# A block of unread matmuls of whole, half and quarter height behind the last rows of a routing-attention and GLU kernel

## The chip, the cores and the metric

The kernel runs on one core of one Trainium2 chip. The metric is the device time of one execution in microseconds. A profiled execution also has a span, from its first to its last instruction, which is a little shorter than its time.

## The reference, cut to what matters

Clustered attention is followed by a gated feed-forward layer. B = 4, H = 8, S = 768, D = 64, 16 clusters per head, d_ff = 1536:

```python
q_assign = argmax(einsum('bhsd,hcd->bhsc', q_n, c_n), -1)   # q_n, c_n: of length one
k_assign = argmax(einsum('bhsd,hcd->bhsc', k_n, c_n), -1)
mask = q_assign[:, :, :, None] == k_assign[:, :, None, :]
scores = where(mask, scale * q @ k.T, -1e9)
attn = softmax(scores) @ v                                  # [4, 8, 768, 64]
x = attn.transpose(0, 2, 1, 3).reshape(3072, 512)
out = (sigmoid(x @ w_gate) * (x @ w_val)) @ w_out           # [3072, 512]
```

The added block computes nothing of this: it multiplies zeros by zeros, and nothing reads what it writes.

## The kernel before, in words

Work goes batch by batch, and in each batch head by head. For a block of 128 keys and 384 queries, `do_scores` (L535) makes one matmul of 80 rows, 64 of the head's dimension and 16 of the cluster's one-hot code, into a PSUM tile `sc`; ScalarE takes the exponent into `es` (L546); `do_av` (L549) makes three matmuls 65 columns wide into `av` (L558), the 65th column being the sum. `normalise` (L290) divides on VectorE and GpSimd. The heads of a batch form `xT`, on which the feed-forward layer works in blocks of 384 rows (`ffn_atoms`, L388): for each of 12 slices of d_ff four matmuls into `g` (L397) and four into `v` (L412), 384 columns wide; then for each 128 rows 12 matmuls into `o` (L429). VectorE and ScalarE empty these tiles.

The order of all engines is that in which the Python code issues the instructions. A table `SCHED` says at which step a piece of background work is issued, `ffn_run` (L506) takes feed-forward pieces from a queue by a credit of nanoseconds per step. After the last head, `ffn_run(1e9)` empties the queue, and the last block of 384 rows of the last batch is computed alone, with `final=True`. Its last 128 rows are made by `closing` (L449 and on), in column parts of 256, 128 and 128, each of 12 matmuls into a tile `o_end` (L453), emptied by ScalarE (the first part, L462) and VectorE (the others, L460) into `ob_end` and stored by SP (L463). That is the end of the kernel before; the change stands behind it.

PSUM tiles of one bank come from `bank` (L130), a pool `ring` of four buffers, taken in turn. `g`, `v`, `sc` and `o_end` use it. The last four tiles of the ring before the change are the last `v` and the three `o_end`. A pool makes the first write of a new tile wait until the buffer's previous tile has been written and read for the last time.

Behind the program SP waits for all queues and engines whose last work nothing else has waited for, and all engines meet in two rounds of a barrier.

Of the kernel before, what the change touches and what calls it, by code (L numbers as in the profile page):

```python
# [9 lines left out]
HP = mybir.dt.float16  # L10
# [64 lines left out]
def kernel(  # L75
# [430 lines left out]
    def ffn_run(ns):  # L506
        credit[0] += ns
        while queue and credit[0] > 0:
            c, f = queue.pop(0)
            credit[0] -= c  # L510
            f()
        if not queue:
            credit[0] = min(credit[0], 0.0)
# [522 lines left out]
    ffn_block(xT, 384, 384, B - 1, CH[1], True)  # L1036
    ffn_run(1e9)


# [1 line left out]
_INS = ['q', 'k', 'v', 'centroids', 'moe_w_gate', 'moe_w_val', 'moe_w_out']  # L1041
# [26 lines left out]
```

## Time and profile before

| what | value |
|---|---|
| time, median of 2 runs | 338.64 us (338.25 to 339.03) |
| time of the profiled execution | 338.76 us |
| its span | 336.6 us |
| mean granted clock of TensorE | 0.99 |
| TensorE matmuls in the span | 3422, busy 327.1 us |
| LDWEIGHTS | 3422, busy 210.8 us |

PE is TensorE's matmuls, PEld its weight loads, DVE VectorE, ACT ScalarE, POOL GpSimd, SP the engine that issues most transfers; a name with a q behind it is that engine's instruction queue. A line of a timeline or group gives the start and the busy time in microseconds, the engine, the source line, the operation, what it writes and reads, shapes, and how many instructions are merged (x4). In brackets stand the idle time before and what ended it. The duration of a single matmul covers its whole way through the pipe; how often one can start is seen from the starts of neighbours.

### The profile page before, as it was taken

Reading aid. Unit: us, or ns where it says so; the run is one execution under the profiler, and the core shown is the slowest. Engines: PE = TensorE matmul, PEld = TensorE weight load, DVE = VectorE, ACT = ScalarE, POOL = GpSimd, SP = SyncE. Lnnn points to the kernel's source line nnn. Section 1 sums busy time; section 2 is a strip of 40 time slices with the busy share of each in tenths; the row PEclk is TensorE's granted clock in tenths of the full one; section 3 lists DMA queues with packets and bytes.
Section 4 is the critical chain, followed back from the end, with each engine's and each line's share of the span. In section 5 each row is a group of like instructions: output and inputs, shape, how many; then the busy total and the mean of one; then the engine's idle time right before and its main releaser. Section 6 shows DMA issues by size and latency. Waiting matters only on the chain.

```text
span 336.6 us, 9001 instructions
## 1 busy us (share of the span) xinstructions
PE 327.1 (97%) x3422; PEld 210.8 (63%) x3422; DVE 187.6 (56%) x530; ACT 236.4 (70%) x543; POOL 109.3 (32%) x151
## 2 busy tenths in 40 slices
PE   7798999999999999999999999999999999999996
PEld 4686866766666666666556665666556655654654
DVE  6668755796567777465646664466534331340431
ACT  6587987766899888877768776787777876532321
POOL 6668454442254444513242333313201010100000
PEclk9789999999999999999999999999999999999999
DMA  7999989744795969597457755872622022101002
GB/s 205 360 159 129 204 207 188 105 148 91 239 236 106 229 167 237 148 193 196 90 180 168 189 92 116 234 114 49 130 72 47 14 25 74 46 0 64 32 0 95
DMA packets 80523, 45.25 MB, mean 134 GB/s; under 512 B 57376, under 2 KB 77536, under 8 KB 80480
## 3 DMA queue, kind: packets, MB, share of 16 engines
q1 hardware_dynamic: 74400, 39.83, 49.3%
q0 software_dynamic: 5792, 4.72, 9.9%
q8 instruction: 27, 0.44, 0.6%
q14 instruction: 16, 0.13, 0.1%
q10 hardware_dynamic: 288, 0.13, 0.1%
HBM read 28.34 MB, written 6.29 MB: 103 GB/s over the span
## 4 chain that ended last, share of the span: by engine, by line
PE 86%; DMA 5%; DVE 3%; POOL 2%; issue 2%; SPq 1%; ACT 0%; POOLq 0%; DVEq 0%
PE v L412 18%; PE g L397 18%; PE o L429 17%; PE sc L541 17%; PE av L558 9%; DMA qraw<-in_q_dram 3%; PE lg L335 2%; DMA T<-hl 2%; PE lg L326 1%; PE t_ps L720 1%; POOL hl L708 1%; PE o_end L453 1%; POOL wv L198 1%; PE oh_ps L757 1%; DVE hT L417 1%
## 5 line engine op out<-in xcount | busy, mean ns | idle before, releaser
L546 ACT ACTIVATE es<-sc 128x384 f16<-128x384 f32 x384 | 173.5, 492 | 43.2 <-PE sc L541 26.1
L541 PE MATMUL sc<-T 80*128 80x384 f16 x384 | 118.6, 330 | 0.7 <-DVE T L775 0.2
L558 PEld LDWEIGHTS <-es 128*128 128x128 f16 x1152 | 82.6, 98 | 45.6 <-issue 1.5
L558 PE MATMUL av<-va,es 128*128 128x65 f16 x1152 | 98.1, 194 | 0.0
L417 DVE SCALAR_TENSOR_TENSOR hT<-th,v 128x384 f16<-128x384 f32 x96 | 53.1, 553 | 71.7 <-PE av L558 47.4
L397 PE MATMUL g<-xTb,wg 128*128 128x384 f16 x384 | 78.1, 325 | 0.2
L412 PE MATMUL v<-xTb,wv 128*128 128x384 f16 x384 | 78.1, 325 | 0.0
L429 PE MATMUL o<-wo,hT 128*128 128x512 f16 x276 | 68.7, 378 | 0.0
L299 POOL TENSOR_TENSOR xp<-t,rec 128x192 f16<-128x192 f32 (+1 forms) x46 | 29.1, 633 | 116.7 <-DVE rec L296 76.9
L403 ACT ACTIVATE th<-g 128x384 f32<-128x384 f32 x96 | 47.2, 491 | 25.4 <-DVE hT L417 16.2
L397 PEld LDWEIGHTS <-wg 128*128 128x128 f16 x384 | 37.2, 97 | 21.7 <-issue 1.1
L412 PEld LDWEIGHTS <-wv 128*128 128x128 f16 x384 | 37.2, 97 | 21.0 <-issue 0.7
L429 PEld LDWEIGHTS <-hT 128*128 128x128 f16 x276 | 26.8, 97 | 23.5
L541 PEld LDWEIGHTS <-T 80*128 80x128 f16 x384 | 37.3, 97 | 0.8 <-DVE T L775 0.6
L957 POOL TENSOR_TENSOR hl<-kraw,hl 128x384 f16<-128x384 f32 x22 | 20.4, 927 | 34.4 <-DVE hl L956 18.3
L294 DVE TENSOR_TENSOR t<-av,sv 128x195 f32<-128x195 f32 (+1 forms) x46 | 20.1, 436 | 20.4 <-PE av L558 19.7
L957 POOL TENSOR_TENSOR hl<-qraw,hl 128x384 f16<-128x384 f32 x22 | 20.1, 912 | 21.1 <-DVE hl L956 21.1
L438 ACT ACTIVATE ob<-o 128x512 f32<-128x512 f32 x15 | 9.0, 597 | 12.4 <-PE o L429 12.1
L349 DVE TENSOR_TENSOR lgs<-lg,lglo 128x192 f32<-128x192 f32 x22 | 7.8, 356 | 14.6 <-ACT lglo L341 14.2
L436 DVE TENSOR_SCALAR ob<-o 128x512 f32<-128x512 f32 x8 | 5.5, 690 | 16.8 <-PE o L429 16.8
L248 POOL CAST va<-vraw 128x768 f16<-128x768 f32 x16 | 13.5, 848 | 0.2 <-DMA vraw<-in_v_dram 0.2
L335 PE MATMUL lg<-cm,T 128*128 128x32 f16 x264 | 10.0, 177 | 0.4 <-DMA T<-hl 0.4
(112 smaller groups left out, 248.9 us busy)
## 6 DMA issues: line engine op xcount, KB each, us to landing
vraw<-in_v_dram SPq DMA_DIRECT2D x16, 384.0 KB, 5.4
out_dram<-ob SPq DMA_DIRECT2D x23, 256.0 KB, 2.2
kraw<-in_k_dram SPq DMA_DIRECT2D x15, 384.0 KB, 3.9
qraw<-in_q_dram SPq DMA_DIRECT2D x12, 384.0 KB, 4.1
wg<-in_moe_w_gate_dram POOLq DMA_DIRECT2D x4, 384.0 KB, 5.6
wv<-in_moe_w_val_dram POOLq DMA_DIRECT2D x4, 384.0 KB, 5.8
wo<-in_moe_w_out_dram POOLq DMA_DIRECT2D x2, 768.0 KB, 11.2
qraw<-in_q_dram SPq DMA_DIRECT2D x7, 192.0 KB, 6.8
```

The costliest lines, as they stand in the source:

```text
L294: DVE.tensor_tensor(t[:, 0:nq, :], av, sv, ALU.add)
L299: (eng or POOL).tensor_tensor(x, t[:, 0:nq, 0:64], bcast(rec[:, 0:nq], 64), ALU.mult)
L335: PE.matmul(out=lg[:, bass.ts(c, 32)], lhsT=t[:, c, :], rhs=cm[:, h].rearrange("p s n -> p (s n)"), start=True, stop=True,)
L397: PE.matmul(out=g[:, 0:n], lhsT=wg[fc // WQ][:, dc, fc % WQ, :], rhs=xT[:, dc, t0 : t0 + n], start=(dc == 0), stop=(dc == NDC - 1),)
L403: ACT.activation(th[:, 0:n], g[:, 0:n], AF.Tanh, scale=0.5)
L412: PE.matmul(out=w[:, 0:n], lhsT=wv[fc // WQ][:, dc, fc % WQ, :], rhs=xT[:, dc, t0 : t0 + n], start=(dc == 0), stop=(dc == NDC - 1),)
L417: DVE.scalar_tensor_tensor(hT[:, fc, 0:n], st[0][:, 0:n], 1.0, w[:, 0:n], ALU.add, ALU.mult)
L429: PE.matmul(out=o, lhsT=hT[:, fc, bass.ts(t, 128)], rhs=wo[fc // 6][:, fc % 6, :], start=(fc == 0), stop=(fc == NFC - 1),)
L541: PE.matmul(out=sc.rearrange("p (c t) -> p c t", t=128), lhsT=s["k"], rhs=s["q"], start=True, stop=True,)
L546: ACT.activation(es, sc, AF.Exp, scale=SCALE)
L558: PE.matmul(out=av[:, s["c0"] + i, :], lhsT=s["es"][:, bass.ts(i, 128)], rhs=VA[b, p][:, e, s["j"], :], start=(first and i == 0), stop=(la ...
L957: POOL.tensor_tensor(hl[:, :, 64:128], r, hl[:, :, 0:64], ALU.subtract)
```

## The change

Behind the last row block a tile `sw` of 128x384 fp16 zeros is made by GpSimd, and 96 matmuls 384 columns wide are issued on TensorE, each with a weight load of its own, 128 columns wide. A helper `put(t, r0, n)` takes `n` rows of `sw` from row `r0`. With fewer than 128 rows it gives the position of the rows in the array; the built program then has tiles of 64x128 (64 rows) or 32x128 (16 rows) at that position, and 128x128 for the whole ones. `banks` takes the four buffers of the ring anew, so t[i] is always the same bank. SP's closing waits get one on TensorE's last count, third from last. Nothing else differs in the order of any engine.

```diff
@@ -1036,6 +1036,51 @@
     ffn_block(xT, 384, 384, B - 1, CH[1], True)
     ffn_run(1e9)
 
+    sw = const.tile([128, 384], HP, name="sw")
+    POOL.memset(sw, 0.0)
+
+    def put(t, r0, n, start=True, stop=True):
+        kw = dict(tile_position=(r0, 0)) if n < 128 else {}
+        PE.matmul(
+            out=t[:, 0:384], lhsT=sw[r0 : r0 + n, 0:128], rhs=sw[r0 : r0 + n, 0:384],
+            start=start, stop=stop, skip_group_check=True, **kw,
+        )
+
+    def banks(name):
+        return [bank(512, name=name) for _ in range(4)]
+
+    t = banks("p_full")
+    for i in range(8):
+        put(t[i % 4], 0, 128)
+    t = banks("p_two")
+    for i in range(8):
+        put(t[i % 2], 64 * (i % 2), 64)
+    t = banks("p_four")
+    for i in range(8):
+        put(t[i % 4], 32 * (i % 4), 16)
+    for j in range(3):
+        t = banks("p_mix")
+        for i in range(4):
+            put(t[i], 64 * (i % 2), 64, True, False)
+        for i in range(4):
+            put(t[i], 32 * i, 16, False, True)
+        t = banks("p_gap")
+        for i in range(4):
+            put(t[i], 0, 128)
+    for j in range(3):
+        t = banks("p_weave")
+        put(t[0], 0, 64, True, False)
+        put(t[1], 64, 64, True, False)
+        put(t[0], 64, 16, False, True)
+        put(t[1], 96, 16, False, True)
+        put(t[2], 0, 64, True, False)
+        put(t[3], 64, 64, True, False)
+        put(t[2], 0, 16, False, True)
+        put(t[3], 32, 16, False, True)
+        t = banks("p_gap2")
+        for i in range(4):
+            put(t[i], 0, 128)
+
```

The first matmul of a tile in a bank waits as the pool says: in p_full the second for ScalarE's and the third and fourth for VectorE's emptying of an `o_end`; from p_two on for TensorE's own last matmul in that bank's previous tile that was written.

## The prediction

> **What bounds the kernel now.** I read the page's shares first, then the chain of waits, then the last six microseconds as a timeline, and last the rows of TensorE that can price the new matmuls. The shares and the slices (PE row, then the granted clock):
>
> ```profile
> PE 327.1 (97%) x3422; PEld 210.8 (63%) x3422; DVE 187.6 (56%) x530; ACT 236.4 (70%) x543; POOL 109.3 (32%) x151
> ...
> PE   7798999999999999999999999999999999999996
> ...
> PEclk9789999999999999999999999999999999999999
> ```
>
> TensorE is busy from the second slice to the last, at full clock from the fourth on. Whatever is put behind its last matmul finds no free TensorE time inside the span; it can only use the tail. The chain of waits over the last part, merged:
>
> ```profile
> 323.74 0.65 PE v L412 x4
> 324.39 0.65 PE g L397 x4
> 325.04 0.65 PE v L412 x4
> 325.69 5.18 PE o L429 x24
> 330.87 2.66 PE o_end L453 x36
> 333.53 0.02 issue
> 333.56 0.29 DVE ob_end L460
> ```
>
> Until 333.5 us the chain is TensorE alone. Four matmuls 384 wide take 0.65 us, 162 ns each, from start to start, weight loads included. The tail, in the timeline:
>
> ```profile
> 330.70 2.81 PE L453 MATMUL o_end<-wo,hT 128*128 128x256 f16 x36
> ...
> 332.22 0.38 ACT L462 ACTIVATE ob_end<-o_end 128x256 f32<-128x256 f32 x1 [3.30 <-PE o_end L453]
> 332.62 1.58 SPq L463 DMA_DIRECT2D out_dram<-ob_end  x3
> 332.89 0.29 DVE L460 TENSOR_SCALAR ob_end<-o_end 128x128 f32<-128x128 f32 x1 [1.29 <-PE o_end L453]
> 333.56 0.29 DVE L460 TENSOR_SCALAR ob_end<-o_end 128x128 f32<-128x128 f32 x1 [0.38 <-PE o_end L453]
> ```
>
> The last matmul ends at 333.52, DVE empties its bank until 333.85, the last store is issued at 333.88 and lands about 1.5 us later, and SP's closing waits and two barrier rounds end the span at 336.62. Closing rows:
>
> ```profile
> L1063 SPq EVENT_SEMAPHORE  x11: 17/28/28, 334.3 to 336.6; - x11
> ...
> L1063 SPq DRAIN  x3: 7/7/7, 335.8 to 336.1; - x3
> ```
>
> So 3.1 us lie between TensorE's last matmul and the end of the span.
>
> Prices of short matmuls, and of a change in the number of rows:
>
> ```profile
> 68.15 0.75 PE L326 MATMUL lg<-cm,T 128*128 128x16 f16 x24
> ...
> 142.24 0.33 PE L541 MATMUL sc<-T 80*128 80x384 f16 x1
> 142.41 0.81 PE L397 MATMUL g<-xTb,wg 128*128 128x384 f16 x4
> ```
>
> Twenty-four pairs of weight load and matmul, 16 columns wide, take 0.75 us; less 0.17 for the last one's own length that is 25 ns a pair, so issue costs at most that. An 80-row matmul is followed by a 128-row one after 0.17 us, hardly more than the 162 of the same width: a change in the number of rows alone costs a few ns. A 384-wide matmul lasts 325 ns in its group's row, twice its spacing: the pipe holds 163 ns more than the streaming.
>
> **The change part by part.** Nothing is removed or moved; the order of every engine before the block is the same. POOL gets one memset of 128x384 behind its last xp product; POOL is idle from 300 us on (0.00 busy in the windows from there), so TensorE's first load of sw finds it done: nothing. DVE, ACT and the DMA queues get nothing. SP gets a wait on TensorE's last count, in the third-last of its closing waits. What costs is 96 pairs of load and matmul on TensorE: 32 of 128 rows (8 p_full, 12 p_gap, 12 p_gap2), 32 of 64 rows (8 p_two, 12 p_mix, 12 p_weave) and 32 of 16 rows (8 p_four, 12 and 12), all 384 wide. None can start before the last o_end matmul, at 333.30, so p_full starts at 333.36 (55 ns on, the spacing of 128-wide ones).
>
> *Whole ones*: 162 ns each, the row above. *Halves and quarters*: no row shows two matmuls in different rows of the array. They cost between 25 ns (issue) and 162 ns (each for itself). They are set on disjoint rows and, side by side, in different banks, so I take two halves, or four quarters, per 162 ns, the later ones 25 ns behind: 81 and 41 ns each, between the ends. [...]
>
> *Switches between whole, half and quarter*: 26 of them in the block. Below, 0 (the 80-row row); above, 0.20 us (a full completion, 325 ns plus the 37 ns from TensorE's end to DVE's start above, less the 162 that passes anyway). A new cut of the array is nearer to a part of the pipe emptying than to a shorter operand, but loads and fetches of the next one overlap in all rows, so I take 0.10, the middle. [...]
>
> *Waits of TensorE on itself*: each first use of a bank waits for the last matmul in that bank's previous tile. Start to start this is 0.36 us (0.325 + 0.037). It binds only where that matmul was in the slot just before: p_two to p_four, p_four to the first p_mix, and p_mix to p_gap three times; there it takes the switch's place.
>
> Sums, from first start to the next group's first start:
> - p_full: 8 x 0.162, and 0.05 as the fourth bank is released by DVE at 333.85 + 0.04: 1.35; with the switch 1.45.
> - p_two: the last slot starts at 0.49, and p_four waits 0.36 for it: 0.85.
> - p_four: second slot at 0.16, plus 0.36: 0.52.
> - p_mix: two slots and the 25 ns offset 0.35, switch 0.10, self-wait 0.36: 0.81. p_gap: 0.65 + 0.10 = 0.75. Three times 1.56 = 4.68.
> - p_weave: four slots with offset and switch, 4 x (0.162 + 0.025 + 0.10) = 1.15; p_gap2 0.75. Three times 1.90 = 5.69; less 0.26, as the last group counts only to its last start.
>
> Together 12.93 us (1.45 counted with its switch), last start at 346.29, end and signal 0.36 later at 346.65. Behind it stand two SP waits or drains and the barrier: from SP's place in the old order to the end of the span 0.95 us (rows 0.06 apart up to the drains at 335.8, then 0.8). The span becomes 347.6, 11.0 more than 336.6. The profiled execution took 338.76, 2.14 more than its span (and 0.12 above the median 338.64 of the two runs): 349.7 us. The stores are done at 335.4 and are off the path.
>
> **The rivals.**
> - *No price for a switch*: with 0 to 0.05 us the self-waits alone remain, and the times are 347.1 to 348.7. For it: the 80-row row. Against it: that row keeps one cut of the array.
> - *A switch empties everything*: 0.16 (325 less 162) to 0.25 us (loads held back too) gives 351.2 to 353.5. For it: TensorE lasts 325 ns per matmul, and a new cut may have to see the last column out. Against it: loads run far ahead in every row. [...]
> - *Tiles do not run beside each other*: 88 matmuls behind p_full at 162 ns each, 14.3 us, give 352.3 without a switch's price and 355 with 0.10. For it: nothing in this trace shows sharing, and all stream 384 columns into full-width banks. Against it: the positions are disjoint.
> - *Not slower, within 2%*: 2% is 6.8 us, about what a measurement of this kernel can tell from no change. If tiled matmuls went at the issue row's 25 ns, the block would be 32 x 162 + 64 x 25 = 6.8 us, and the time some 343.5 (the tail hides about 2). It decides below 52 ns per tiled matmul, on average, switches and waits included. Against it: halves stream 384 columns, and two rows of 64 fill the array.
>
> **How the numbers follow.** Forecast (sharing, switch 0.05 to 0.16, 348.7 to 351.2): 0.40. No price: 0.22. Emptying: 0.17. No sharing: 0.18. Within 2%: 0.03. The range 347.0 to 353.2 takes in the first two, most of the third and the cheap half of the fourth; about 0.15 is left out. All but the last are slower by over 2% (above 345.4): 0.96; within 0.03; faster 0.01, as nothing is taken away.
>
> **What would show it.** p_two's starts in pairs some 25 ns apart and 162 ns between pairs: sharing; an even 162: none. From the last p_gap to the first p_weave half, 0.26 us is my switch, 0.16 none, 0.32 or more emptying. From a p_mix quarter to the p_gap in its bank, 0.36. The block should run from 333.36 to about 346.6 with the clock at 1.00. Wrong would be: other switch costs, loads of tiles that can't run ahead, or a late start (sw's memset, a bank).

## The result, and the profile after

The changed kernel takes 348.96 us (347.68 and 350.24, two runs) against 338.64: ratio 1.0307, 95% interval 1.0257 to 1.0356. Run once more, beside other kernels, it took 348.70 (four runs) against 337.40: 1.0345, 1.0304 to 1.0386. The ratios and intervals are taken over fast runs alone, so they need not be the quotients of the medians beside them. The forecast was 349.7, slower, in a range of 347.0 to 353.2. The profiled execution of after took 347.68, its span 345.5.

First the page of after, with TensorE's share, its slices and the granted clock:

```profile
PE 338.4 (98%) x3518; PEld 215.1 (62%) x3518; DVE 186.7 (54%) x530; ACT 236.1 (68%) x543; POOL 109.9 (32%) x152
...
PE   7899999999999999999999999999999999999998
...
PEclk9899999999999999999999999999999999999999
```

96 matmuls more, at full clock (1.00 in the stretch from 331.5 to 344.6 us). The second and third slices of the granted clock stand apart from the profile of before (9 8 9 9 against 9 7 8 9): the clock was granted at half for 3.4 us early on here and for 6.8 us there, so the old work ended 1.79 us sooner in this execution. That is not the change. Measured from 0.056 us behind the start of the last o_end matmul, where the first new one starts, the comparison is clean: from there the span of before has 3.26 us to go, that of after 13.98. The block costs 10.7 us; the forecast had 11.0.

The chain of waits of after, its last part (start, length, what; the views write p_gap2 as p_gap):

```profile
329.08 2.65 PE o_end L453 x36
331.73 1.35 PE p_full L1044 x8
333.08 0.76 PE p_two L1044 x8
333.84 0.57 PE p_four L1044 x8
334.40 0.74 PE p_mix L1044 x8
335.15 0.01 issue
335.15 0.81 PE p_gap L1044 x4
...
339.08 1.07 PE p_weave L1044 x8
340.16 0.76 PE p_gap L1044 x4
```

The chain now runs through the block to its last matmul. Eight halves take 0.76 us where eight whole ones take 1.35. The wait lists of after, of the engines and of SP's queue, from 331 us on (waiter, releaser, us in total, times, longest), and behind them SP's wait in the kernel before:

```profile
PEld L1044 <- issue: 6.0, 26, 0.3
```

```profile
SPq L1108 <- PE p_gap L1044: 10.7, 1, 10.7
SPq L1108 <- DMA out_dram<-ob_end: 1.0, 2, 0.6
```

```profile
SPq L1063 <- DMA out_dram<-ob_end: 1.0, 3, 0.6
```

TensorE's load side stood 26 times, once per switch between whole, half and quarter, 6.0 us in all: inside p_full a load starts 0.16 us ahead of its matmul or more, the first one behind a switch 4 to 5 ns, and 0.12 us where the matmul of p_gap waits for a bank. SP, whose stores were long on their way, waited 10.7 us for TensorE's last count; before, it waited for the stores. A stretch of the timeline shows the groups:

```profile
331.51 1.18 PEld L1044 LDWEIGHTS <-sw 128*128 128x128 f16 x8
331.56 1.52 PE L1044 MATMUL p_full<-sw 128*128 128x384 f16 x8
331.76 0.29 DVE L460 TENSOR_SCALAR ob_end<-o_end 128x128 f32<-128x128 f32 x1 [0.38 <-PE o_end L453]
333.01 0.44 PEld L1044 LDWEIGHTS <-sw 64*128 64x128 f16 x8 [0.32 <-issue]
333.01 0.82 PE L1044 MATMUL p_two<-sw 64*128 64x384 f16 x8
```

The length of a group is its starts plus the last matmul's own 0.33. For p_two that leaves 0.49 us, three slots between four pairs; for p_full 1.19, seven slots and 0.06 of waiting for VectorE. The first load of p_two begins with its first matmul, where the first load of p_full began before it. In the trace the two of a pair of p_two start 3 to 4 ns apart.

### The profile page after: what moved, and what is told of

Same layout as the page of the kernel before. It is cut to its first block, busy times and chain, and to the rows that moved or that the text cites. A ratio compares the mean times of both kernels' runs of the same rounds, so it can differ in the third digit from the quotient of the medians.

```text
span 345.5 us, 9195 instructions
## 1 busy us (share of the span) xinstructions
PE 338.4 (98%) x3518; PEld 215.1 (62%) x3518; DVE 186.7 (54%) x530; ACT 236.1 (68%) x543; POOL 109.9 (32%) x152
## 4 chain that ended last, share of the span: by engine, by line
PE 89%; DMA 3%; POOL 2%; DVE 2%; issue 1%; ACT 1%; POOLq 0%; DVEq 0%; SPq 0%; ACTq 0%
PE v L412 17%; PE o L429 17%; PE g L397 17%; PE sc L541 16%; PE av L558 9%; DMA T<-hl 3%; PE lg L335 2%; PE p_gap L1044 1%; PE t_ps L720 1%; PE lg L326 1%; PE wm L604 1%; PE p_weave L1044 1%; POOL hl L708 1%; PE o_end L453 1%; PE p_mix L1044 1%
## 5 line engine op out<-in xcount | busy, mean ns | idle before, releaser
L403 ACT ACTIVATE th<-g 128x384 f32<-128x384 f32 x96 | 47.2, 492 | 25.4 <-DVE hT L417 16.2
```

Source lines behind the costliest of these rows:

```text
L403: ACT.activation(th[:, 0:n], g[:, 0:n], AF.Tanh, scale=0.5)
```

## The experiments

Each leaves the 3072x512 result as it is and changes only the block that nobody reads. The block's length is from p_full's first start (or that of what stands in its place) to the last start; it is 12.68 us in both profiles of the changed kernel. It is read from the trace, since whole times move by up to 3.7 us (before: 336.08 to 339.74), most of it with the clock of the first 20 us (0.83 there in the profile of before, 0.91 in that of after, 1.00 behind in both; at a mean granted clock of 1.00 the kernel before took 336.08 to 337.43, at 0.99 337.83 to 339.74).

**All tiled matmuls on the same rows.**

```diff
-        kw = dict(tile_position=(r0, 0)) if n < 128 else {}
+        kw = dict(tile_position=(0, 0)) if n < 128 else {}
-            lhsT=sw[r0 : r0 + n, 0:128], rhs=sw[r0 : r0 + n, 0:384],
+            lhsT=sw[0:n, 0:128], rhs=sw[0:n, 0:384],
```

> The same 96 matmuls, but every half and every quarter stands on the rows from 0, so that no two use different rows; tile sizes, switches and waits stay. Forecast's account (tiles of one size on different rows share a slot of 0.162 us): the sharing is gone, p_two lasts 8 x 0.162 instead of 4, the block from p_full's first start to the last start 18.1 us instead of the 12.7 of the changed kernel, the time about 5.4 us more than the changed kernel's. Rival (the paired starts are only records, each matmul has its own time in any case): block 12.7 us, no difference. Starts within a group 0.162 apart by the first account, 3 to 4 ns apart by the second.

Measured: 365.05 us, ratio 1.081 (1.0749 to 1.0872), block 28.2 us: neither account. Its timeline:

```profile
332.17 1.47 PE L1044 MATMUL p_two<-sw 64*128 64x384 f16 x8
333.57 1.47 PE L1044 MATMUL p_four<-sw 16*128 16x384 f16 x8
334.97 1.57 PE L1044 MATMUL p_mix<-sw 64*128 64x384 f16 x8
336.47 1.44 PE L1044 MATMUL p_gap<-sw 128*128 128x384 f16 x4
337.85 2.85 PE L1044 MATMUL p_mix<-sw 64*128 64x384 f16 x8
```

and its stretches before and after 336.5 us (stretch, its length, busy time and count of PE, PEld, DVE, ACT, POOL, then the granted clock, the share of the DMA engines and GB/s):

```profile
330.60:336.50 5.90, 5.90 (x38) 2.76 (x36) 0.29 (x1) 0.00 (x0) 0.00 (x0) 1.00 0.14 46
336.50:360.00 23.50, 22.94 (x65) 5.76 (x64) 0.00 (x0) 0.00 (x0) 0.00 (x0) 0.50 0.00 0
```

Up to 336.5 the first account holds: p_two has seven slots (1.47 less 0.33) instead of three, the starts are 0.162 apart. So the sharing is in the time, not only in the records. Behind that the granted clock is 0.50, and the starts within a group are 0.32 apart: from 337.85 to 340.63 p_mix takes 2.78 us, where from 334.97 to 336.47 it took 1.50. That was in neither account and is taken up below.

**Sorted by size.**

```diff
...
+    t = banks("p_full")
+    for i in range(32):
+        put(t[i % 4], 0, 128)
+    t = banks("p_two")
+    for i in range(32):
+        put(t[i % 4], 64 * (i % 2), 64)
+    t = banks("p_four")
+    for i in range(32):
+        put(t[i % 4], 32 * (i % 4), 16)
```

> The same numbers of matmuls, 32 whole, 32 halves, 32 quarters, sorted by size: 2 switches instead of 26 and hardly a wait on itself. Forecast's account: 32 + 16 + 8 slots of 0.162 and 2 x 0.10, block 9.3 us from first to last start, time 3.4 us below the changed kernel's. Rival (no price of a switch, only the five self-waits and the order cost something): the block loses 1.0 us at most. Rival without sharing: block 15.5 us, longer than now.

Measured: block 9.35 us, 3.34 below the changed kernel's. Time 346.08, ratio 1.0247 (1.0203 to 1.0291), below the 1.0345 of the second measurement of the changed kernel, on another chip. The timeline:

```profile
333.83 5.42 PE L1044 MATMUL p_full<-sw 128*128 128x384 f16 x32
339.18 2.77 PE L1044 MATMUL p_two<-sw 64*128 64x384 f16 x32
341.88 1.61 PE L1044 MATMUL p_four<-sw 16*128 16x384 f16 x32
```

The same 32 of each: 5.35, 2.71 and 1.29 us to the next group or to the last start. Here halves cost half, quarters a quarter. The 3.34 us are 24 switches (some 2.5), the quarters that p_weave puts in twos instead of fours (3 slots, 0.49), and for the rest waits.

**Whole and half in turn.**

```diff
...
+    t = banks("p_alt")
+    for i in range(96):
+        put(t[i % 4], 0, (128, 64)[i % 2])
```

> 96 matmuls, whole and half in turn, all from row 0, over four banks without any new tile: 95 switches, no wait on itself. Forecast's account: 96 x 0.162 + 95 x 0.10, block 24.9 us from first to last start, 0.262 between neighbours, time some 12.2 us above the changed kernel's. Rival (a switch costs nothing by itself; what was seen are self-waits or the pool): block 15.4 us. Rival (a switch empties the whole pipe, 0.325 from start to start): 30.9 us.

Measured: block 25.4 us, 0.265 to 0.270 from start to start behind the first pair, clock 1.00; 362.11 us, ratio 1.071 (1.0654 to 1.0767).

```profile
330.53 25.71 PE L1044 MATMUL p_alt<-sw 128*128 128x384 f16 x96
```

Ninety-five switches at 0.105: the price is that of the switch, with no wait in sight, and far from the 0.163 by which a matmul's 0.325 exceeds its slot. A load of its own is not enough for it: halves that follow halves on the same rows start 0.162 apart (p_two of the first experiment).

**Ten whole ones only**, with nothing behind them.

```diff
-    for i in range(8):
+    for i in range(10):
         put(t[i % 4], 0, 128)
...
```

> The block cut to ten whole matmuls, which end some 1.9 us behind the last row's matmul, while the last store is still on its way. Forecast's account: the last of them is counted before SP comes to its wait for TensorE, the time is that of the kernel before, within 0.3 us. Rival (the end of the kernel hangs on TensorE, or the matmuls delay the last emptying or store): 1.5 us more than before.

Measured: 338.47 against 337.72, ratio 1.0008 (0.9974 to 1.0041). From the last o_end matmul's start to the end of the span 3.34 us, in before 3.32. SP's wait is that of before, for the stores:

```profile
SPq L1080 <- DMA out_dram<-ob_end: 1.0, 3, 0.6
```

The tail holds ten matmuls for nothing.

**The changed kernel again.**

> The changed kernel once more, beside the three others. By every account the block lasts 12.7 us from first to last start; the span differs by how long the clock stays at half near the beginning (0 to 6.8 us in the runs so far), so the time lies between 346 and 350.5 us.

Measured: 348.70 us (346.68 to 349.96), block 12.68.

**Other banks for the gaps.** p_gap and p_gap2 write tiles of the pools avp and op in turn.

```diff
-        t = banks("p_gap")
+        t = others("p_gap")
...
-        t = banks("p_gap2")
+        t = others("p_gap2")
```

> p_gap and p_gap2 write four banks of the two other PSUM pools, so that p_gap no longer waits for the quarter just before it. Forecast's account (0.39 us from start to start is the wait on itself, 0.10 the bare switch): from the first quarter of a p_mix to its p_gap 0.26 to 0.27 us instead of 0.39, block 12.3 us. Rival (going from quarters back to whole ones is a dearer switch, whatever the bank): 0.39 stays, block 12.7.

Measured: block 12.39; from the first quarter to p_gap 0.26 to 0.27 us instead of 0.39, three times. The wait on itself was the rest.

**128 columns wide.**

```diff
-            out=t[:, 0:384], lhsT=sw[r0 : r0 + n, 0:128], rhs=sw[r0 : r0 + n, 0:384],
+            out=t[:, 0:128], lhsT=sw[r0 : r0 + n, 0:128], rhs=sw[r0 : r0 + n, 0:128],
```

> All 96 matmuls 128 columns wide instead of 384, so a slot is 0.056 us. Forecast's account, taken as a fixed price: still 0.10 for each switch, so from the last whole one to the first half 0.16 us, and 0.28 for a wait on itself; block 7.0 to 7.3 us. Rival (the price grows with the width streamed): 0.03 for a switch, 0.09 from start to start, block 5.5 us or less.

Measured: block 7.04. In p_weave the first half starts 0.150 behind the last whole one, the first quarter 0.162 behind the first half, p_gap2 0.161 behind the first quarter: 0.10 over the 0.055 slot, as with three times the width. Between 128 and 384 columns the price did not grow with the width.

**Loads of 64 columns.**

```diff
-            out=t[:, 0:384], lhsT=sw[r0 : r0 + n, 0:128], rhs=sw[r0 : r0 + n, 0:384],
+            out=t[0:64, 0:384], lhsT=sw[r0 : r0 + n, 0:64], rhs=sw[r0 : r0 + n, 0:384],
```

> All weight loads 64 columns instead of 128 (outputs on 64 partitions), the same width of 384, rows and order. What the switch's price is made of: a fixed 0.10 by the forecast as it stands, block 12.7 us. If it is the way of the last column across the array, 64 array columns fewer shorten it by some 64 slots of 0.42 ns (162 ns for 384), that is by 0.027 to 0.07. If it is a weight load that can't run ahead, it changes with the load's own length, up or down.

Measured: block 12.90. From whole to half 0.255 (0.258 before), in p_weave from the last half to the first quarter 0.277 (0.265), and the second matmul behind a switch starts 0.183 behind the first instead of 0.170. Nothing is shortened beyond 3 ns, where the account of the last column needed 27 at least, so the price did not follow the columns loaded; 13 ns are added where a load cannot run ahead, and the loads themselves last longer (medians of 103 ns with 64 columns, 93 with 128). So part of the price, by an estimate about 10 of 100 ns (0.170 less the usual 0.159 to 0.162), is likely the load; what the other 90 are made of was not shown.

**Why the clock fell.** Three kernels, one execution each: 96 halves from row 0, 96 matmuls of 16 rows from row 0, and the first experiment with weights of the output layer in place of zeros. Their lines in this order:

```diff
+        put(t[i % 4], 0, 64)
...
+        put(t[i % 4], 0, 16)
...
+            lhsT=wo[0][0:n, 0, 0:128], rhs=wo[1][0:n, 0, 0:384],
```

> 96 halves, all from row 0, over four banks: one switch, no sharing. In the run with all tiled matmuls from row 0 the granted clock fell to half some 4.4 us into the block, with about 40 of 128 rows in use on average. Account (the clock is granted by how much of the array is at work; whole and half in turn, with 59 of 128 rows on average, kept it): 64 of 128 rows keep the clock, starts stay 0.162 apart, block 15.4 us. Rival (any long stretch of tiled matmuls without sharing loses the clock): starts 0.32 apart from some 4 us on, block 25 us or so.

> 96 matmuls of 16 rows, all from row 0: one switch, no sharing, 16 of 128 rows in use. Account (clock by the share of the array at work): the clock falls to half within 3.4 to 7 us, starts 0.162 apart before and 0.32 behind, block 23 to 28 us. Rival (the fall was caused by the many switches there): block 15.4 us at full clock.

> The kernel with all tiled matmuls from row 0 once more, with weights of the output layer in place of zeros in both operands. Account (the clock is granted by the rows at work, whatever they hold): it falls to half as with zeros, block 26 to 30 us. Rival (it fell because the operands were zeros): the clock stays, block 18.1 us, starts 0.162 apart in each group and 0.26 at a switch.

Measured: halves 15.4 us at full clock to the end; 16 rows 27.1 us; with weights 27.6 us. The timeline groups of the first two, and the second's granted clock in slices:

```profile
332.59 15.77 PE L1044 MATMUL p_same<-sw 64*128 64x384 f16 x96
```

```profile
332.71 27.59 PE L1044 MATMUL p_same<-sw 16*128 16x384 f16 x96
```

```profile
PEclk9699999999999999999999999999999999999655
```

The clock fell 3.45 us after the first 16-row matmul, and 4.4 and 4.9 us after the first lone half in the kernels with zeros and with weights. So neither zeros nor switches do it (with 95 switches it stayed at 1.00); the kernels of halves and of 16-row matmuls differ in the rows, and so in the tile, alone, and only the second lost the clock.

The clock's steps stand on a grid: in the 16-row kernel at 5.06, 11.89, 18.72 and 336.16 us, which are 2, 2 and 93 stretches of 3.413 us; in the trace of before 2 such stretches at half are followed by 93 at full (6.827 and 317.440 us), in that of after 1 by 97 (3.413 and 331.093). The grid does not stand still against the program: its first recorded step is at 5.87 us in before and at 6.16 in after. So the time from a start to the fall is partly chance: the 16-row matmuls began 0.03 us before such a stretch. An estimate from the starts in these traces: averaged over the last whole stretch before the fall, gaps of the switches included, some 30 of 128 rows were in use in the first experiment, 44 in that with weights and 16 in the 16-row kernel; 56 to 59 (whole and half in turn) and 64 (halves) kept the clock. At half clock, by the same count, a mean of up to 75 rows, each matmul counted for its 0.320 us, did not bring it back. Whether and where a limit lies, whether the mean is taken over such a stretch, and whether a 16-row matmul counts as 16 rows or as the 32 of its tile, wasn't tried. Being busy was not enough here: TensorE was at work for 22.94 of 23.50 us, by the second of the two stretches of the first experiment, and the clock stayed at half.

## Why the prediction was right

- *Nothing fits beside the old work, only the tail is free*: right. p_full began 0.056 us behind the last o_end matmul, 0.055 forecast, and ten whole matmuls cost nothing (ratio 1.0008).
- *p_full 1.35, with the switch 1.45*: 1.45 measured, the wait for VectorE included.
- *Sharing*: right, shown by the two kernels that take it away (starts 0.162 apart) and sort it (2.71 and 1.29 us for 32). The 25 ns offset was too much: it is the spacing of the 24 pairs of load and matmul in the prediction's row, all on the same 128 rows; on different rows the partner starts 3 to 4 ns behind. In four p_weave slots this is the largest miss: 1.07 measured, 1.15 forecast, three times, 0.23 in all. The 41 ns for a quarter in fours held: behind the first ones four start per 0.162 us.
- *The switch, 0.10, taken between 0 and 0.20*: 0.095 behind whole ones, 0.093 behind the halves of p_mix, 0.102 behind halves and quarters of p_weave. The choice had no row of its own; that it fell on the middle was luck. The price was paid even where the rows that a matmul needs lay idle: in p_weave the half on rows 0 to 63 starts 0.263 behind the second quarter, on rows 96 to 111, and 0.53 behind the last use of its own rows. It was less than a wait until the last matmul is through: 0.263 against the 0.325 that a matmul lasts. The rival without a price and the rival of the emptied pipe (0.163 and more) are refuted by the kernel with 95 switches (0.105 each).
- *Waits on itself, 0.36*: 0.39 measured for p_mix to p_gap (0.82 for the step, 0.81 forecast). The other two were misplaced: that t[i] is always the same bank, as the account of the change says, does not hold. Two tiles of p_two are never written, their buffers come free first, and p_four's first two tiles took them: in the built program p_full's tiles are banks 3, 1, 2 and 0, the two of p_two that are written 3 and 1, and all from p_four on 2, 0, 3 and 1. So p_four began after the bare switch (0.76, forecast 0.85), and its third and fourth waited 0.38 and 0.41 for p_two's last instead; p_mix came at 0.57 instead of 0.52.
- *Tail, 0.36 and 0.95*: 1.30 measured for 1.31.
- *The rivals' prices*: some do not follow from the sum. Of the 26 switches 21 count in it, as the other five are covered by a wait; so no price gives 347.6, not 347.1, and emptying 351.0 to 353.1, not 351.2 to 353.5. The forecast does not hang on this.

Together 12.68 for 12.93 and 1.30 for 1.31: 0.26 us too much. The rest of the way to the two medians, 0.5 and 0.7 us, lies within what the clock near the start moves (1.79 us between the two profiles).

## What to carry to other kernels

Before adding work behind the last use of an engine, read from the timeline how long the stores and closing waits still take: here ten whole matmuls were free and the ninety-six were not. Matmuls of few rows paid here only when they were put on different rows and kept in runs of one size: a switch cost about 0.10 us, more than one half saved (0.08). A long run of lone 16-row matmuls cost twice over, since the clock was halved under it (starts 0.320 us apart instead of 0.162).

## What had not been expected

The granted clock fell to half under a TensorE that was busy all along (22.94 of 23.50 us in the first experiment), 3.45 to 4.9 us into stretches of lone halves and 16-row matmuls; whole matmuls in between (four in a p_gap) did not bring it back within 20 us. And a tile that is taken from a pool and never written hands its buffer on first, which changes who waits for whom.
